# An identity made on GpSimd, first transposes in the order of the loads, larger q and k loads, and half of v's loads issued by GpSimd

## The chip, the cores and the metric

The kernel runs on one core of a Trainium2 chip. The metric is device time in microseconds (us) of one execution; lower is better. The kernel before took 1226.99 us (median of three runs, 1224.92 to 1231.88).

## What is computed

Attention over chunks of 64 tokens, then a mixture of eight experts in which tokens are assigned in the order of their logits up to a capacity, then a dense layer of three weights. Only the first part is touched by the change:

```python
# q, k, v: (8 batches, 8 heads, 576 tokens, 64), float32; 9 chunks of 64 tokens
scores = scale * q_c @ k_c.T            # within each chunk of 64 tokens
attn   = softmax(scores)                # max subtracted, sum + 1e-9
x      = (attn @ v_c)                   # to (4608 tokens, 512)
logits = x @ w_gate                     # 4608 x 8
# tokens take experts in the order of the sorted logits, 576 per expert
y[mask_e]  = relu(x[mask_e] @ w1[e]) @ w2[e]
out = max(relu(y @ m1), y @ m2, y @ m3) @ m_out
```

## The kernel before

The 72 chunks (8 batches of 9) are worked on in 36 iterations of two chunks, all eight heads at once. Four iterations share one unit `u` of eight chunks: there are nine units. For each unit, q and k are loaded by 128 partitions (16 per chunk, four tokens in each, 1 KB in one piece per head); v by 64 partitions per chunk, with 256 bytes in one piece. Since a unit of eight chunks can begin in one batch and end in the next, a q or k load of a unit is issued in one or two pieces (`pieces`, L37). `load_qk(u, part)` (L46) loads four heads of k or q or both; `load_v(u, part)` (L58) loads two chunks of v in four transfers of 64 KB, of which one is issued by GpSimd where `u` is above 0.

TensorE needs q and k with the head's 64 elements on the partitions. `trans(nm, u, n)` (L85) turns two of the eight heads by four transposes against the identity `ident`, into one of two PSUM buffers `pT`; `evac` (L97) copies the result in two halves, by ScalarE and VectorE, into `QT`. Transposes `n` = 0 and 1 read heads 0 to 3, `n` = 2 and 3 heads 4 to 7.

Before the loop, unit 0 is loaded (`load_qk(0, 0)`, `load_qk(0, 1)`), then parts of v of unit 0 and of q and k of unit 1 by turns (L78 to L83); the eight transposes of unit 0 run with k and q by turns (L204 to L208). In the loop (L213), iteration `i` loads a quarter of v of unit `i // 4 + 1` and a quarter of q and k of unit `i // 4 + 2`, and runs the scores of `i` (L112), its maximum, difference and exponential, the transposes of one quarter of unit `i // 4 + 1`, the attention times v of `i - 1` (L161), and scaling, store and transposes of x of `i - 2` (L168, L170, L179). Logits come every fourth iteration (L191, L200). q's and k's buffers are double, so a load of unit `u + 1` has to wait until unit `u - 1` is transposed.

The order of the work on each engine is that of the program; each engine works through its own list in order. SyncE issues q, k and most of v; GpSimd issues the stores of x and a quarter of v; ScalarE issues `w_gate` and two transfers for the identity.

The identity is made in `Router.__init__` (L295 to L298): VectorE writes a matrix with ones in its first column, ScalarE stores it to memory (`unit`) and reads it back with a row pitch of 127, which puts the ones on the diagonal. `Router.consts` (L300) has GpSimd make the router's constants; among them `dif` (L322), column minus row, and its comparison with zero (L334). It is called before `attention`, so it comes ahead of the memsets of two of v's three buffers (L76, L77) in GpSimd's list.

Of the kernel before, what the change touches and what calls it, by code (L numbers as in the profile page):

```python
# [7 lines left out]
F32 = mybir.dt.float32  # L8
# [5 lines left out]
OP = mybir.AluOpType  # L14
# [3 lines left out]
B, H, S, D = 8, 8, 576, 64  # L18
# [5 lines left out]
NU = G // 4  # L24
# [1 line left out]
BIG = 1.5e38  # L26


def attention(ctx, tc, q, k, v, wg_in, xd, L, ident, early, mark):

    nc = tc.nc
    C = ctx.enter_context(tc.tile_pool(name="ac", bufs=1))
    P = ctx.enter_context(tc.tile_pool(name="aw", bufs=2))
    PS = ctx.enter_context(tc.tile_pool(name="aps", bufs=2, space=PSUM))
    QK, QT, KBT, PT, PSS, MX, A, R, PA, AT, PX, X, PY, XT, LS = ({} for _ in range(15))

    def pieces(u):  # L37
        r, j = [], 0
        while j < 8:
            b, c = divmod(8 * u + j, 9)  # L40
            n = min(8 - j, 9 - c)
            r.append((j, n, b, c))
            j += n
        return r

    def load_qk(u, part, nms="kq"):  # L46

        for nm in nms:
            if part == 0:
                QK[nm, u] = P.tile([128, H, 4 * D], F32, name="in" + nm)  # L50
            src, h = (k if nm == "k" else q), 4 * part
            for j, n, b, c in pieces(u):
                nc.sync.dma_start(
                    QK[nm, u][16 * j:16 * (j + n), h:h + 4],
                    bass.AP(tensor=src.tensor, offset=src.offset + (b * H + h) * S * D + c * 64 * D,
                            ap=[[4 * D, 16 * n], [S * D, 4], [1, 4 * D]]))

    def load_v(u, part):  # L58

        t = VB[u % 3]  # L60
        for j in (2 * part, 2 * part + 1):
            b, c = divmod(8 * u + j, 9)
            for s in range(2):
                (nc.gpsimd if u and j % 2 and s else nc.sync).dma_start(
                    t[s * 64:(s + 1) * 64, j, :, s, :],
                    bass.AP(tensor=v.tensor, offset=v.offset + b * H * S * D + s * S * D + c * 64 * D,
                            ap=[[D, 64], [2 * S * D, 4], [1, D]]))

    load_qk(0, 0)
    load_qk(0, 1)  # L70
    wg = C.tile([128, 4, 32], F32, name="wg")
    nc.vector.memset(wg, 0.0)
    nc.scalar.dma_start(wg[:, :, :8], wg_in.rearrange("(a p) e -> p a e", p=128))
    VB = [C.tile([128, 8, 4, 2, 64], F32, name="vb%d" % i) for i in range(3)]
    for t, eng in ((VB[0], nc.vector), (VB[1], nc.gpsimd), (VB[2], nc.gpsimd)):
        eng.memset(t[0:64, :, :, 1, :], 0.0)  # L76
        eng.memset(t[64:128, :, :, 0, :], 0.0)  # L77
    load_v(0, 0)  # L78
    load_qk(1, 0)
    load_v(0, 1)  # L80
    load_v(0, 2)
    load_qk(1, 1)
    load_v(0, 3)  # L83

    def trans(nm, u, n):  # L85

        mark(nm + "T")
        if n == 0:
            QT[nm, u] = P.tile([128, 4, 8, 64], F32, name=nm + "T")
        pt = PS.tile([128, 2, 2, 128], F32, name="pT")  # L90
        PT[nm, u, n] = pt
        for a in range(2):
            for w in range(2):
                h = 4 * (n // 2) + 2 * a + n % 2
                nc.tensor.transpose(pt[:, a, w, :], QK[nm, u][:, h, w * 128:w * 128 + 128], ident)  # L95

    def evac(nm, u, n, r, eng):  # L97
        mark(nm + "E")
        s, h0 = n % 2, 2 * (n // 2)
        src = PT[nm, u, n][r * 64:r * 64 + 64].rearrange("p a w t -> p a t w")  # L100
        dst = QT[nm, u][s * 64:s * 64 + 64, h0:h0 + 2].rearrange("p a j (i w r) -> p a (j i) w r", w=2, r=2)[:, :, :, :, r]
        (nc.vector.tensor_copy if eng else nc.scalar.copy)(dst, src)

    def scores(g):
        mark("scores")
        u, h = divmod(g, 4)
        PSS[g] = PS.tile([128, 2, 512], F32, name="pS", bufs=1)[:, :, :256].rearrange("p s (a i) -> p a s i", a=4)
        for hp in range(4):
            for c in range(2):
                for s in range(2):  # L110
                    o, to = slice(s * 64, s * 64 + 64), slice(c * 64, c * 64 + 64)
                    nc.tensor.matmul(PSS[g][to, hp, s], QT["q", u][o, hp, 2 * h + c], QT["k", u][o, hp, 2 * h + c],  # L112
                                     start=True, stop=True, tile_position=(s * 64, c * 64))
# [51 lines left out]
    def scale(g):  # L165
        mark("scale")
        X[g] = P.tile([128, 8, 64], F32, name="x", bufs=3)
        nc.vector.tensor_tensor(X[g], PX[g].rearrange("p a (s i) -> p (a s) i", s=2),  # L168
                                R[g][:, :, None].to_broadcast([128, 8, 64]), op=OP.mult)
        nc.gpsimd.dma_start(xd[g * 128:(g + 1) * 128, :], X[g].rearrange("p h d -> p (h d)"))  # L170
# [30 lines left out]
        nc.vector.tensor_reduce(L[:, 4 * j + w0:4 * j + w1, :],  # L201
                                pl[:, w0:w1, :, :8].rearrange("p w a e -> p w e a"), op=OP.add, axis=AX.X)

    for n in range(4):  # L204
        for nm in "kq":
            trans(nm, 0, n)
            for r in range(2):
                evac(nm, 0, n, r, r)  # L208

    def on(j):  # L210
        return 0 <= j < G

    for i in range(G + 2):  # L213
        u, n = i // 4 + 1, i % 4
        tr = u < NU
        if tr:
            load_v(u, n)
        if u + 1 < NU:
            load_qk(u + 1, n // 2, "kq"[n % 2])
        if on(i):  # L220
            scores(i)
        if on(i - 2):
            scale(i - 2)
        if on(i):
            smax(i)
        if on(i - 1):
            att_t(i - 1)
            att_c(i - 1)
            sums(i - 1, 0)
        if tr:  # L230
            trans("q", u, n)
            evac("q", u, n, 0, 0)
            trans("k", u, n)
            evac("k", u, n, 0, 0)
        if on(i):
            ssub(i)
        if tr:
            evac("k", u, n, 1, 1)
        if on(i):
            expo(i)  # L240
        if i == G + 1:
            logit1(8, 0, 3)
        if on(i - 2):
            x_t(i - 2)
        if tr:
            evac("q", u, n, 1, 0)
        if on(i - 1):
            pv(i - 1)
            sums(i - 1, 1)
            sums(i - 1, 2)  # L250
        if i >= 7 and (i - 4) % 4 == 3 and i < G:
            logit2((i - 4) // 4)
        if i >= 6 and (i - 3) % 4 == 3 and i < G:
            logit1((i - 3) // 4)
        if on(i - 2):
            x_c(i - 2)
        if i == G + 1:
            early()
            logit2(8, 0, 3)
            logit1(8, 3, 4)  # L260
            logit2(8, 3, 4)
# [3 lines left out]
class Clock:  # L265
# [4 lines left out]
    def __init__(s):  # L270
        s.pe = s.dve = 0
# [12 lines left out]
class Router:  # L284

    def __init__(s, ctx, tc, mark, scratch):
        s.tc, s.mark, s.clock = tc, mark, Clock()
        nc = s.nc = tc.nc  # L290
        C = s.C = ctx.enter_context(tc.tile_pool(name="rc", bufs=1))
        s.L = C.tile([128, G, E], F32, name="L")
        s.ident = C.tile([128, 128], F32, name="ident")

        nc.vector.memset(s.ident, 0.0)  # L295
        nc.vector.memset(s.ident[:, 0:1], 1.0)
        nc.scalar.dma_start(scratch, s.ident)
        nc.scalar.dma_start(s.ident, bass.AP(tensor=scratch.tensor, offset=scratch.offset, ap=[[127, 128], [1, 128]]))  # L298

    def consts(s, tmp):  # L300
        nc, C = s.nc, s.C

        def io(shape, pat, base=0, cm=0, name=None):
            t = C.tile(shape, F32, name=name)
# [9 lines left out]
                       allow_small_or_imprecise_dtypes=True)  # L314
# [3 lines left out]
                       allow_small_or_imprecise_dtypes=True)  # L318
        s.row = io([128, 1], [[0, 1]], cm=1, name="row")
        s.w8 = io([128, E], [[-1, E]], base=E, name="w8")  # L320
        dif = tmp.tile([128, 128], F32, name="dif")
        nc.gpsimd.iota(dif, pattern=[[1, 128]], base=0, channel_multiplier=-1, allow_small_or_imprecise_dtypes=True)  # L322
        s.tri = C.tile([128, 128], BF, name="tri")
        nc.gpsimd.tensor_scalar(s.tri, dif, 0.0, None, op0=OP.is_gt)

# [298 lines left out]
def kernel(ctx, tc, q, k, v, w_gate, w1, w2, m1, m2, m3, m_out, out, mark=lambda n: None):  # L624
    nc = tc.nc
    ctx.enter_context(tc.manual_schedule())
    dram = ctx.enter_context(tc.tile_pool(name="dram", bufs=1, space=bass.MemoryType.DRAM))
    xd = dram.tile([NT, DM], F32, name="xd")
# [2 lines left out]
    mo = dram.tile([F2, DM], F32, name="mo")  # L631
    wda = dram.tile([9 * 128, 2, 768], F32, name="wda")
    wdb = dram.tile([9 * 128, 2, 1024], F32, name="wdb")
    unit = dram.tile([128, 128], F32, name="unit")
    rt = Router(ctx, tc, mark, unit)
    with ExitStack() as c2:
        consts = c2.enter_context(tc.tile_pool(name="tmp", bufs=1))
        rt.consts(consts)
        attention(c2, tc, q, k, v, w_gate, xd, rt.L, rt.ident, rt.early, mark)
    ring = ctx.enter_context(tc.tile_pool(name="ring", bufs=10))  # L640
    P = rt.W = ctx.enter_context(tc.tile_pool(name="mw", bufs=1))
    c3 = ExitStack()
# [300 lines left out]
    for r in range(E):  # L943
# [53 lines left out]
        for d in range(4):  # L997
# [3 lines left out]
            for hf in range(2):  # L1001
                tk = slice(hf * 288, hf * 288 + 288)
                n = 0
# [193 lines left out]
```

## Time and profile before

| what | value |
|---|---|
| median of three runs | 1226.99 us |
| profiled execution | 1226.38 us |
| its span, first to last instruction | 1224.6 us |
| busy in the span | TensorE 1173.0 us (96%), VectorE 846.3 (69%), ScalarE 415.2 (34%), GpSimd 263.8 (22%) |
| granted TensorE clock, mean | 0.989 |
| HBM traffic | 197 GB/s over the span |

Busy time counts an engine as busy while an instruction of it runs; the span is cut from the first to the last instruction, and the execution's time is 1.8 us longer. Attention fills the first 170 us of the span, the router's first round the time up to about 205 us, the experts and the dense layer the rest.

### The profile page before, as it was taken

To read this page: it belongs to the slowest core of one execution; us is meant where nothing else is said; L and a number is where in the kernel's file an instruction comes from. 1 tells how busy PE (TensorE), PEld (TensorE's weight loads), DVE (VectorE), ACT (ScalarE), POOL (GpSimd) and SP (SyncE) were. 2 spreads that over 40 slices of the span, in tenths; PEclk is the share of its full clock that TensorE was granted. 3 is DMA by queue.
4 is the path that set the end of the run, shared out by engine and by line. 5 is a ranking of instruction groups with operands and counts; after the bars stand their busy time and mean duration, and the time that the engine had idled before them with its cause. 6 is when DMAs were issued, how large, how long until landed. Compare 5 with 4: busy or idle time off the path is not lost.

```text
span 1224.6 us, 23432 instructions
## 1 busy us (share of the span) xinstructions
PE 1173.0 (96%) x9485; PEld 1093.1 (89%) x9485; DVE 846.3 (69%) x1684; ACT 415.2 (34%) x673; POOL 263.8 (22%) x381
## 2 busy tenths in 40 slices
PE   5999978999999999999899999999999999999998
PEld 4787745899999998999899998998998998998996
DVE  5888876877788889888954466566566565565561
ACT  4888832233333332334423113113113113113111
POOL 6232211010135343544760001001001001002002
PEclk9999987999999999999999999999999999999999
DMA  9999915263655565757674564674663763763651
GB/s 210 250 262 248 228 53 164 80 227 96 202 179 191 169 202 173 233 167 255 210 257 176 215 253 174 232 263 150 258 256 139 266 241 138 267 252 135 220 202 52
DMA packets 148781, 243.11 MB, mean 199 GB/s; under 512 B 39490, under 2 KB 111938, under 8 KB 141762
## 3 DMA queue, kind: packets, MB, share of 16 engines
q1 hardware_dynamic: 129234, 184.05, 47.2%
q0 software_dynamic: 14016, 47.98, 11.6%
q10 hardware_dynamic: 5424, 9.59, 2.2%
q8 instruction: 75, 1.23, 0.4%
q14 instruction: 32, 0.26, 0.1%
HBM read 195.12 MB, written 46.47 MB: 197 GB/s over the span
## 4 chain that ended last, share of the span: by engine, by line
PE 41%; issue 36%; DVE 10%; DMA 8%; POOL 2%; SPq 1%; ACT 1%; POOLq 1%; DVEq 0%; ACTq 0%
PE acc L1007 14%; PE acc L964 13%; DMA inq<-in_q_dram 4%; PE py L1045 2%; POOL out_dram L1129 2%; DMA vb<-in_v_dram 2%; DVE chunk L693 2%; PE px L1045 2%; PE pz L1045 2%; PE pX L161 1%; PE pxt L747 1%; PE pT L95 1%; PE po L1121 1%; DVE hlo L984 1%; DVE ge L469 1%
## 5 line engine op out<-in xcount | busy, mean ns | idle before, releaser
L1007 PE MATMUL acc<-hhi,chunk 128*128 128x288 f32 x1024 | 211.1, 300 | 1.2 <-DVE hlo L984 1.2
L964 PE MATMUL acc<-xhi,chunk 128*128 128x288 f32 x1024 | 206.4, 300 | 3.9 <-DVE hlo L984 3.2
L964 PEld LDWEIGHTS acc<-xhi,chunk 128*128 128x128 f32 x1024 | 160.3, 188 | 6.0 <-DVE hlo L984 4.1
L1007 PEld LDWEIGHTS acc<-hhi,chunk 128*128 128x128 f32 x1024 | 162.7, 188 | 1.8 <-DVE hlo L984 1.5
L1007 PE MATMUL acc<-hlo,chunk 128*128 128x288 f32 x512 | 151.0, 295 | 1.0 <-DVE hlo L984 0.9
L1121 PE MATMUL po<-chunk,h 128*128 128x512 f32 x648 | 149.3, 390 | 0.0
L1129 POOL DMA_INDIRECT out_dram<-ot,ia x36 | 35.4, 985 | 521.1 <-ACT ot L1127 519.6
L1121 PEld LDWEIGHTS po<-chunk,h 128*128 128x128 f32 x648 | 121.5, 188 | 24.8
L964 PE MATMUL acc<-xlo,chunk 128*128 128x288 f32 x512 | 143.0, 295 | 0.0
L1045 PE MATMUL px<-xb,wa 128*128 128x384 f32 x648 | 129.9, 334 | 0.7 <-ACT ys L1014 0.7
L1045 PE MATMUL py<-xt,wb 128*128 128x384 f32 x648 | 129.8, 334 | 0.0
L1045 PEld LDWEIGHTS px<-xb,wa 128*128 128x128 f32 x648 | 113.9, 188 | 1.3 <-ACT ys L1014 1.0
L1045 PEld LDWEIGHTS py<-xt,wb 128*128 128x128 f32 x648 | 114.0, 188 | 0.5
L1066 ACT CAST h<-best 128x384 fp32r<-128x384 f32 x72 | 37.0, 514 | 198.0 <-DVE best L1064 121.3
L1007 PEld LDWEIGHTS acc<-hlo,chunk 128*128 128x128 f32 x512 | 96.0, 188 | 1.4 <-DVE hlo L984 1.4
L964 PEld LDWEIGHTS acc<-xlo,chunk 128*128 128x128 f32 x512 | 93.4, 188 | 0.0
L976 ACT ACTIVATE hhi<-acc 128x576 fp32r<-128x576 f32 x64 | 41.8, 652 | 144.6 <-PE acc L964 121.4
L693 DVE TENSOR_TENSOR chunk<-raw,chunk 128x1024 fp32r<-128x1024 f32 x67 | 88.2, 1320 | 2.7 <-ACT chunk L686 2.7
L1081 ACT COPY tmp<-px 128x384 f32<-128x384 f32 x54 | 25.9, 480 | 146.2 <-PE px L1045 146.2
L723 POOL DMA_INDIRECT xg<-xd,idx x40 | 41.9, 1049 | 153.7 <-DVE ohe L612 65.5
L686 ACT CAST chunk<-raw 128x1024 fp32r<-128x1024 f32 x67 | 69.7, 1046 | 8.9 <-ACT ys L1014 6.9
L984 DVE SCALAR_TENSOR_TENSOR hlo<-acc,hhi 128x576 fp32r<-128x576 f32 x64 | 48.2, 753 | 34.5 <-ACT hhi L976 34.3
(207 smaller groups left out, 2012.4 us busy)
## 6 DMA issues: line engine op xcount, KB each, us to landing
wb<-wdb SPq DMA_DIRECT2D x54, 1024.0 KB, 4.9
wa<-wda SPq DMA_DIRECT2D x54, 768.0 KB, 5.9
raw<-in_moe_w_dram SPq DMA_DIRECT2D x64, 512.0 KB, 4.5
xd<-x POOLq DMA_DIRECT2D x36, 256.0 KB, 5.3
yd<-ys ACTq DMA_DIRECT2D x32, 288.0 KB, 3.1
wdb<-pair POOLq DMA_DIRECT2D x18, 512.0 KB, 5.2
yraw<-yd SPq DMA_DIRECT2D x12, 768.0 KB, 7.5
vb<-in_v_dram SPq DMA_DIRECT2D x112, 64.0 KB, 5.8
```

What stands on the lines that cost most here:

```text
L686: nc.scalar.copy(hi, raw)
L693: nc.vector.tensor_tensor(lo, raw, hi.bitcast(F32), op=OP.subtract)
L723: nc.gpsimd.indirect_dma_start(out=g, out_offset=None, in_=xd[:, :], in_offset=bass.IndirectOffsetOnAxis(ap=rt.idx[r][:, t:t + 1], axis=0))
L964: nc.tensor.matmul(acc[:, hf, :288], w[a][:, dc, o:o + 128], x[:, dc, tk], start=n == 0, stop=n == 11)
L976: nc.scalar.activation(hv, acc[:, :, :288], AF.Relu)
L984: nc.vector.scalar_tensor_tensor(hl[:, f].rearrange("p (a t) -> p a t", a=2), acc[:, :, :288], 0.0, hv.bitcast(F32), op0=OP.max, op1=OP.su ...
L1007: nc.tensor.matmul(acc[:, hf, :288], w[a][:, f, :], x[:, f, tk], start=n == 0, stop=n == 23)
L1045: nc.tensor.matmul(dst, w[:, dc, o, a], XO[x][:, c, dc], start=start and n == 0, stop=stop and n == 5, skip_group_check=True)
L1066: nc.scalar.copy(hpart(g, i, j)[0], M)
L1081: nc.scalar.copy(U[g, 1], XB[g])
L1121: nc.tensor.matmul(PO[t], h[:, x, t % 6 * 128:t % 6 * 128 + 128], w[a][:, f % 2], start=f == 0 and n == 0, stop=f == 5 and n == 2)
L1129: st = nc.gpsimd.indirect_dma_start(out=out, out_offset=bass.IndirectOffsetOnAxis(ap=ia[:, t:t + 1], axis=0), in_=ot, in_offset=None)
```

## The change

The identity is made by GpSimd as the first thing after its start: an iota of column minus row and a comparison with zero (`unit`). The round trip through memory goes, and the other constants (`consts`) are called from inside `attention`, after the memsets of v's buffers. `load_qk` now takes one of q and k, a first head and a number of heads: unit 0 and 1 are still loaded by four heads, later units by eight at once, k in the first and q in the third iteration of four. Unit 1's second half moves ahead of the third quarter of unit 0's v. In `load_v`, both transfers of the upper half of the partitions are issued by GpSimd where `u` is above 0, two of four. The first transposes run as k 0, k 1, q 0, q 1, k 2, k 3, q 2, q 3.

```diff
-    def load_qk(u, part, nms="kq"):
-        for nm in nms:
-            if part == 0:
-                QK[nm, u] = P.tile([128, H, 4 * D], F32, name="in" + nm)
-            src, h = (k if nm == "k" else q), 4 * part
-            for j, n, b, c in pieces(u):
-                nc.sync.dma_start(
-                    QK[nm, u][16 * j:16 * (j + n), h:h + 4],
...
+    def load_qk(nm, u, h, n):
+        if h == 0:
+            QK[nm, u] = P.tile([128, H, 4 * D], F32, name="in" + nm)
+        src = k if nm == "k" else q
+        for j, m, b, c in pieces(u):
+            nc.sync.dma_start(
+                QK[nm, u][16 * j:16 * (j + m), h:h + n],
...
-                (nc.gpsimd if u and j % 2 and s else nc.sync).dma_start(
+                (nc.gpsimd if u and s else nc.sync).dma_start(
...
-    load_qk(0, 0)
-    load_qk(0, 1)
+    for h in (0, 4):
+        for nm in "kq":
+            load_qk(nm, 0, h, 4)
     wg = C.tile([128, 4, 32], F32, name="wg")
     nc.vector.memset(wg, 0.0)
-    nc.scalar.dma_start(wg[:, :, :8], wg_in.rearrange("(a p) e -> p a e", p=128))
     VB = ...
+    nc.scalar.dma_start(wg[:, :, :8], wg_in.rearrange("(a p) e -> p a e", p=128))
+    consts()
     load_v(0, 0)
-    load_qk(1, 0)
+    for nm in "kq":
+        load_qk(nm, 1, 0, 4)
     load_v(0, 1)
+    for nm in "kq":
+        load_qk(nm, 1, 4, 4)
     load_v(0, 2)
-    load_qk(1, 1)
     load_v(0, 3)
...
-    for n in range(4):
+    for n in (0, 2):
         for nm in "kq":
-            trans(nm, 0, n)
-            for r in range(2):
-                evac(nm, 0, n, r, r)
+            for i in (n, n + 1):
+                trans(nm, 0, i)
+                for r in range(2):
+                    evac(nm, 0, i, r, r)
...
-        if u + 1 < NU:
-            load_qk(u + 1, n // 2, "kq"[n % 2])
+        if u + 1 < NU and n % 2 == 0:
+            load_qk("kq"[n // 2], u + 1, 0, 8)
...
-        nc.vector.memset(s.ident, 0.0)
-        nc.vector.memset(s.ident[:, 0:1], 1.0)
-        nc.scalar.dma_start(scratch, s.ident)
-        nc.scalar.dma_start(s.ident, bass.AP(tensor=scratch.tensor, offset=scratch.offset, ap=[[127, 128], [1, 128]]))
+    def unit(s, tmp):
+        s.dif = tmp.tile([128, 128], F32, name="dif")
+        s.nc.gpsimd.iota(s.dif, pattern=[[1, 128]], base=0, channel_multiplier=-1, allow_small_or_imprecise_dtypes=True)
+        s.nc.gpsimd.tensor_scalar(s.ident, s.dif, 0.0, None, op0=OP.is_equal)
...
-        rt.consts(consts)
-        attention(c2, tc, q, k, v, w_gate, xd, rt.L, rt.ident, rt.early, mark)
+        rt.unit(consts)
+        attention(c2, tc, q, k, v, w_gate, xd, rt.L, rt.ident, lambda: rt.consts(consts), rt.early, mark)
```

## Rows read from the trace of the kernel before

**Rows 1.** Stretches: us, busy us (instructions) by engine, clock, DMA share, GB/s.
```profile
40.00:130.00 90.00, 86.39 (x1453) 71.51 (x1452) 77.87 (x159) 77.75 (x136) 25.79 (x44) 1.00 1.14 252
...
175.00:200.00 25.00, 17.36 (x149) 8.45 (x150) 17.18 (x77) 2.98 (x3) 1.54 (x2) 0.50 0.22 69
```

**Rows 2.** Chain of waits: start us, us, what (a DMA lasts to its landing).
```profile
0.77 4.04 DMA ink<-in_k_dram
...
4.82 6.04 DMA vb<-in_v_dram
10.86 1.09 PE pT L95 x4
...
13.38 1.13 PE pT L95 x4
```

**Rows 3.** Timeline of ScalarE, start: start us, us, instruction.
```profile
5.04 0.34 ACTq L298 DMA_DIRECT2D ident<-unit  x1
```

**Rows 4.** Waits of SyncE, 0 to 20 us: us, times, longest.
```profile
SPq L53 <- DMA ident<-unit: 3.6, 1, 3.6
```

**Rows 5.** Timeline of TensorE [idle <-releaser]; last, its waits, 30 to 152 us.
```profile
37.53 0.63 PE L95 MATMUL pT<-ident,inq 128*128 128x128 f32 x4 [0.88 <-PE pA L148]
...
48.50 0.69 PE L112 MATMUL pS<-kT,qT 64*64 64x64 f32 x32
...
132.26 0.69 PE L112 MATMUL pS<-kT,qT 64*64 64x64 f32 x32
...
148.14 0.69 PE L112 MATMUL pS<-kT,qT 64*64 64x64 f32 x32
...
PE pT L95 <- DMA inq<-in_q_dram: 3.1, 5, 1.1
```

**Rows 6.** DMA issues at 2.38 and 31.05: KB, us to landing.
```profile
inq<-in_q_dram SPq DMA_DIRECT2D x1, 512.0 KB, 7.4
...
inq<-in_q_dram SPq DMA_DIRECT2D x1, 384.0 KB, 6.4
```

**Rows 7.** SyncE's timeline from 103 us; last, two steps of the chain there.
```profile
103.22 1.16 SPq L53 DMA_DIRECT2D inq<-in_q_dram  x2
104.42 3.15 SPq L64 DMA_DIRECT2D vb<-in_v_dram  x3
108.47 0.85 SPq L53 DMA_DIRECT2D ink<-in_k_dram  x2
109.37 2.98 SPq L64 DMA_DIRECT2D vb<-in_v_dram  x3
...
103.22 7.83 DMA inq<-in_q_dram
...
111.06 0.60 SPq L64
```

**Rows 8.** Timeline of GpSimd, start.
```profile
3.59 0.23 POOL L322 IOTA dif<- 128x128 f32 x1
...
6.30 0.54 POOL L334 TENSOR_SCALAR blk<-dif 128x128 f32<-128x128 f32 x1
...
18.57 2.14 POOL L64 DMA_DIRECT2D vb<-in_v_dram  x3
```

**Rows 9.** Timeline: VectorE's first copy of a transpose, and later transposes.
```profile
12.63 0.69 DVE L102 COPY kT<-pT 64x512 f32<-64x512 f32 x1 [6.97 <-ACT kT L102]
...
22.50 0.60 PE L95 MATMUL pT<-ident,ink 128*128 128x128 f32 x4
```

**Rows 10.** DMA totals, 3 to 10 us and 17.4 to 18.6 us.
```profile
DMA packets 3596, 2.35 MB, mean 335 GB/s; under 512 B 1377, under 2 KB 3596, under 8 KB 3596
...
DMA packets 918, 0.22 MB, mean 183 GB/s; under 512 B 918, under 2 KB 918, under 8 KB 918
```

**Rows 11.** GpSimd's group of x stores, 40 to 130 us: busy, mean ns | idle before.
```profile
L170 POOL DMA_DIRECT2D xd<-x x22 | 12.4, 561 | 65.7 <-DVE x L168 60.6 <-DMA inq<-in_q_dram 2.6 <-DMA vb<-in_v_dram 2.5
```

**Rows 12.** One stretch between the first loads and the next, as rows 1.
```profile
10.30:13.00 2.70, 1.94 (x8) 1.57 (x8) 0.37 (x1) 0.80 (x2) 2.62 (x8) 1.00 0.36 53
```

More of the change, by code (lines that the diff above doesn't have):

```diff
@@ L26, with attention @@
 BIG = 1.5e38
-def attention(ctx, tc, q, k, v, wg_in, xd, L, ident, early, mark):
+def attention(ctx, tc, q, k, v, wg_in, xd, L, ident, consts, early, mark):
     nc = tc.nc
@@ L44, in pieces @@
         return r
-    def load_qk(u, part, nms="kq"):
-        for nm in nms:
-            if part == 0:
-                QK[nm, u] = P.tile([128, H, 4 * D], F32, name="in" + nm)
-            src, h = (k if nm == "k" else q), 4 * part
-            for j, n, b, c in pieces(u):
-                nc.sync.dma_start(
-                    QK[nm, u][16 * j:16 * (j + n), h:h + 4],
-                    bass.AP(tensor=src.tensor, offset=src.offset + (b * H + h) * S * D + c * 64 * D,
-                            ap=[[4 * D, 16 * n], [S * D, 4], [1, 4 * D]]))
+    def load_qk(nm, u, h, n):
[5 more added lines that the diff above has]
+                QK[nm, u][16 * j:16 * (j + m), h:h + n],
+                bass.AP(tensor=src.tensor, offset=src.offset + (b * H + h) * S * D + c * 64 * D,
+                        ap=[[4 * D, 16 * m], [S * D, n], [1, 4 * D]]))
     def load_v(u, part):
@@ L284, with __init__ @@
 class Router:
-    def __init__(s, ctx, tc, mark, scratch):
+    def __init__(s, ctx, tc, mark):
         s.tc, s.mark, s.clock = tc, mark, Clock()
@@ L293, in __init__ @@
         s.ident = C.tile([128, 128], F32, name="ident")
-        nc.vector.memset(s.ident, 0.0)
-        nc.vector.memset(s.ident[:, 0:1], 1.0)
-        nc.scalar.dma_start(scratch, s.ident)
-        nc.scalar.dma_start(s.ident, bass.AP(tensor=scratch.tensor, offset=scratch.offset, ap=[[127, 128], [1, 128]]))
+    def unit(s, tmp):
+        s.dif = tmp.tile([128, 128], F32, name="dif")
+        s.nc.gpsimd.iota(s.dif, pattern=[[1, 128]], base=0, channel_multiplier=-1, allow_small_or_imprecise_dtypes=True)
+        s.nc.gpsimd.tensor_scalar(s.ident, s.dif, 0.0, None, op0=OP.is_equal)
     def consts(s, tmp):
-        nc, C = s.nc, s.C
+        nc, C, dif = s.nc, s.C, s.dif
         def io(shape, pat, base=0, cm=0, name=None):
@@ L320, in consts @@
         s.w8 = io([128, E], [[-1, E]], base=E, name="w8")
-        dif = tmp.tile([128, 128], F32, name="dif")
-        nc.gpsimd.iota(dif, pattern=[[1, 128]], base=0, channel_multiplier=-1, allow_small_or_imprecise_dtypes=True)
         s.tri = C.tile([128, 128], BF, name="tri")
@@ L633 @@
     wdb = dram.tile([9 * 128, 2, 1024], F32, name="wdb")
-    unit = dram.tile([128, 128], F32, name="unit")
-    rt = Router(ctx, tc, mark, unit)
+    rt = Router(ctx, tc, mark)
     with ExitStack() as c2:
         consts = c2.enter_context(tc.tile_pool(name="tmp", bufs=1))
-        rt.consts(consts)
-        attention(c2, tc, q, k, v, w_gate, xd, rt.L, rt.ident, rt.early, mark)
+        rt.unit(consts)
+        attention(c2, tc, q, k, v, w_gate, xd, rt.L, rt.ident, lambda: rt.consts(consts), rt.early, mark)
     ring = ctx.enter_context(tc.tile_pool(name="ring", bufs=10))
```

## The prediction

> **What bounds the kernel now.** I read the busy time by stretches first [rows 1]. From 40 to 130 us TensorE is busy 86.39 of 90 us at a granted clock of 1.00. So attention is TensorE's own work wherever nothing holds it up, and the question is only where it is held up: before its first instruction, and in the 3.6 us that are missing from 40 to 130.
>
> The start of the chain of waits [rows 2] shows the first. TensorE's first transposes begin at 10.86 us, although k's first half landed at 0.77 + 4.04 = 4.81. The view calls the transfer between them "vb", but the thing that came late is the identity: ScalarE can only fetch it back from memory from 5.04 on [rows 3], and SyncE, whose next issue uses that fetch's completion semaphore again, waits 3.6 us for "ident" [rows 4]. The first transposes start as it lands.
>
> The second shows in the starts of the scores, one per iteration [rows 5]. Four iterations that nothing delays take 148.14 - 132.26 = 15.88 us. The five groups of four before them, 48.50 to 132.26, take 83.76, which is 4.4 us more than 5 x 15.88; TensorE's waits give the reason, q's loads, 3.1 us in five times, up to 1.1. So loads cost between 3.1 and 4.4 us there; I take 4.3, as no other wait comes near them. At 37.53 there is one more of 0.88: q's piece issued at 31.05 landed 6.4 later, at 37.4 [rows 6].
>
> Why are those loads late? SyncE's list [rows 7] has its answer in one stretch: the load issued at 103.22 lands at 103.22 + 7.83 = 111.05, and at 111.06 SyncE issues again. Between the two it issued exactly eight (two q, three v, two k, one v). Each of SyncE's and ScalarE's issues takes one of eight completion semaphores and waits for the landing of the one eight before. Five issues per iteration at 6 to 8 us each from issue to landing, eight at a time, is 5 x 6.3 / 8 = 3.9 us per iteration, just TensorE's 15.88 / 4 = 3.97. SyncE is therefore never ahead, and any slow landing reaches TensorE.
>
> **The change, part by part.**
>
> *Identity on GpSimd.* Removed: two memsets, two ScalarE issues, the round trip through memory. Added at the head of GpSimd: an iota of 0.23 and a comparison like the one at 6.30, 0.54 [rows 8], done within 2 us even if GpSimd starts 1 us into the span. Then k's landing at 4.81 is the last thing that the first transposes wait for: 10.86 becomes 4.85, **-6.0 us**. The memsets and constants behind it are the same work as before in another order, so GpSimd still comes to its first v load near 18.57 [rows 8]; unit 1's v is used first after iteration 4's scores, so that costs nothing. If GpSimd's constants slowed VectorE's copies beside them, four copies of 0.69 [rows 9] in the path could double, 2.8 us. GpSimd was at work without a break until that v load, beside those same copies, so I take nothing.
>
> *Order of the first transposes.* Two PSUM buffers, and tile j waits for VectorE's copy of tile j-2: 13.38 - 10.86 = 2.5 us per two tiles [rows 2]. That pace stays. From 4.85 the second matrix is wanted at 7.4, the third load at 9.9, the fourth at 12.5; the fourth lands at 2.38 + 7.4 = 9.8 [rows 6], the others in equal steps after 4.81, at about 6.5 and 8.1. The new order costs and gains nothing by itself. The first transposes take 1.1 us per four [rows 2], those at 22.50 0.6 [rows 9]. I let the change of speed move along with them. Should it stay where it is, the first two iterations run slow, up to 4 us (7 us of work, of which half waits for other engines anyway).
>
> *What is late next.* q of the third unit, needed at iteration 4. Without its wait it would be needed at 37.53 - 0.88 - 6.0 = 30.65. When does it come? SyncE's prologue is 4 qk, 4 v, 4 qk, 4 v, 4 qk, 8 v, then 2 v, 2 k, 4 v, 2 q. By issue: the 9th to 12th wait for the landings of the first loads, the last at 9.8, instead of all four for the identity until just before 10.86, so the second unit's first halves are out by about 10.8; then 18 v at 0.65 and 8 qk pieces at 0.5 to 0.55 (0.43 to 0.65 each in [rows 7]) come to 15.9: q is out at about 26. It moves twice the bytes of the piece that landed 6.4 later [rows 6], so 32. By bytes: 6.3 MB of q and k at the 335 GB/s that k and q alone reached and 1.8 MB of v at 183 [rows 10] are 18.8 + 10.0 us, from 3.2 on (the first landing less its 1.6): 32.0. Both say 32, a wait of 1.4. Place 37.53 moves to 32.1: **-5.4 us** are left of the 6.0. The range of this step is 30.65 (nothing waits) to 35.5 (the same 8.1 MB at the 252 GB/s of rows 1, 32.3 us).
>
> *Eight heads at once, half of v from GpSimd.* SyncE's issues per four iterations fall from 20 (12 v, 8 qk pieces) to 12 (8 v, 4 pieces of double bytes): 12 x 0.65 = 7.8 us of 15.88, and eight in flight now reach over two and a half iterations. The transfers must still fit: per iteration 524 KB of q and k at 335 GB/s is 1.56 us, 262 KB of v at 183 is 1.43, 262 KB of x in packets no smaller than q's is at most 0.78 at 335 [rows 10]; together 3.77 against TensorE's 3.97. GpSimd's v loads rise from four to eight per group: 8 x 0.71 (2.14 for three in [rows 8]) + 4 x 0.561 [rows 11] = 7.9 us of 15.88. They stand in the queue between one x store and the next; the store waits for VectorE anyway (60.6 us in 22 times), so 1.4 us of issues before it are hidden; uncovered they would cost at most the 0.7 added per iteration. Then q is needed whole two iterations after its place in the program, where now its halves have three. But SyncE is held only by the buffer of two units before, free one iteration ahead of the group, and by then has 7.8 us of issues to do in 15.9: q goes out about 1 us into the group, lands by 12 and is needed at 17. So the stalls go: **-4.3 us**. Bounds: 0 (all stay) to -4.7.
>
> [...] The DMA queues' share reads 1.14 from 40 to 130 us [rows 1]: no free engine is visible. [...] The row on eight in flight says that bandwidth was not what was short; the fit of 3.77 in 3.97 decides, and it is close.
>
> *After attention* all moves along. The granted clock is 0.50 from 175 to 200 us [rows 1], while the router keeps TensorE waiting. If its fall and rise do not move along exactly, 4 us more or less of TensorE's work there at the other level make up to 2 us either way; I take 0.
>
> **Sum.** -5.4 - 4.3 = -9.7 on a span of 1224.6. The profiled execution took 1226.4, so 1216.7; the median shown, 1226.99, is 0.6 above it. I say **1217**.
>
> **Rivals.**
>
> *Half of it.* The start's gain is eaten at iteration 4: q lands at 35 or later, or the first iterations stay slow. Then -1.5 to -2.5 there, -4.3 later: about 1220.5. For it: q's bytes are due 5.4 us sooner at rates met only without a mix. Against: 2.7 us from 10.3 to 13.0 ran at 53 GB/s [rows 12], an empty stretch that the identity alone made.
>
> [...]
>
> *q whole comes late in every group (slower).* Place: the wait of the first transpose of each unit. If SyncE does not get ahead and issues q in iteration 2 of 4, it has two iterations and 1.1 us, 9.0 us, to land. Seven loads are concerned; with x us of lateness each, 7x stands against the 9.7: it is slower than before from x = 1.4, that is a landing 10.4 us after issue. The longest now is 7.8 for half the bytes, plus 1.6 for the rest at 335 GB/s and 0.6 for the second issue: 10.0, just short; at 12 us x = 3, and 1226.4 - 9.7 + 21 = 1238. Against: 12 issues instead of 20, so SyncE has time to be ahead.
>
> **How the numbers follow.** A measurement of this kernel tells about 0.5% (6 us) from no change. Forecast 0.56 (own range 1213.5 to 1220); half of it 0.20, split evenly between faster and same; engines bound 0.17, same; q late 0.07, slower. Faster 0.67 (0.56 + 0.10, and a little), same 0.25, slower 0.08. The range: down to 1212.5 (6.0 + 4.7 kept, 2 us of the clock), up to 1224.5, which takes in the bandwidth case and leaves out the slower one.
>
> **What will show it.** The first transposes begin at 4.9 and the first scores near 14; iteration 4's q transposes at 32, and the waits of transposes for q after that near zero; four iterations take 15.9 throughout; iteration 31's scores begin near 138.4 instead of 148.14; SyncE idle before each k load. Wrong, if q's loads still end TensorE's waits, if groups take over 16.3, or if SyncE's issues still follow the landing of the eighth before.

## The result: slower by 0.85%, and the profile after

The kernel after takes 1237.78 us (median of nine runs, 1234.71 to 1241.09), the kernel before 1226.99 (nine runs, 1224.83 to 1231.88): a ratio of 1.0085, 95% interval 1.0064 to 1.0105. The forecast of 1217 is 21 us off, and the time lies outside its range. The profiled execution took 1241.09 us, the longest of the nine; its span is 14.6 us longer than that of before. The page's totals for it:

```profile
span 1239.2 us, 23433 instructions
...
PE 1178.7 (95%) x9485; PEld 1099.2 (89%) x9485; DVE 850.3 (69%) x1682; ACT 414.8 (33%) x673; POOL 282.8 (23%) x414
...
PEclk8799996899999999999999999999999999999999
```

TensorE is busy 5.7 us more with the same work, so part of the loss is work at a lower clock: there are dips in the first and second of the 40 slices, where before has none, and in the seventh and eighth, where before has its own in the sixth and seventh. Its timeline (start, us, instruction, idle before and what ended it), beside [rows 5]:

```profile
14.13 1.06 PE L115 MATMUL pS<-kT,qT 64*64 64x64 f32 x18
...
29.42 0.53 PE L115 MATMUL pS<-kT,qT 64*64 64x64 f32 x18
...
42.59 1.08 PE L98 MATMUL pT<-ident,inq 128*128 128x128 f32 x4 [10.87 <-DMA inq<-in_q_dram]
...
47.01 0.69 PE L115 MATMUL pS<-kT,qT 64*64 64x64 f32 x32
...
85.62 0.27 PE L115 MATMUL pS<-kT,qT 64*64 64x64 f32 x2 [1.23 <-issue]
...
160.43 0.69 PE L115 MATMUL pS<-kT,qT 64*64 64x64 f32 x32
```

And the chain of waits, beside [rows 2] (a DMA lasts to its landing):

```profile
0.77 4.30 DMA ink<-in_k_dram
...
5.20 1.10 PE pT L98 x4
...
27.98 0.27 SPq L52
...
28.29 14.16 DMA inq<-in_q_dram
42.45 0.14 issue
42.59 1.94 PE pT L98 x8
```

The starts of the scores of single iterations divide the 14.6 us:

| place | before | after | difference |
|---|---|---|---|
| first scores | 20.08 | 14.13 | -5.95 |
| iterations 0 to 3 (to the start of 4) | 14.27 | 15.29 | +1.0 |
| iteration 4 | 5.64 | 17.59 | +11.95 |
| iterations 5 to 30 (start of 5 to start of 31) | 108.15 | 113.42 | +5.3 |
| after that | | | +2.3 |

The first gain is there. Then TensorE waits 10.87 us for q of the third unit, issued at 28.29 and landed at 42.45, which costs more than was won. Stretches of the kernel after, with the columns of [rows 1]:

```profile
20.00:42.50 22.50, 10.79 (x190) 9.05 (x187) 12.11 (x24) 10.53 (x19) 8.55 (x15) 0.79 1.15 225
...
40.00:46.60 6.60, 4.01 (x24) 3.71 (x26) 0.97 (x3) 2.61 (x5) 0.00 (x0) 0.50 1.18 177
40.00:130.00 90.00, 80.62 (x1282) 66.64 (x1283) 68.04 (x137) 68.83 (x121) 33.82 (x57) 0.96 1.10 232
...
128.70:132.10 3.40, 3.40 (x24) 3.07 (x24) 1.07 (x3) 2.72 (x5) 0.47 (x1) 0.50 0.41 90
...
217.40:224.20 6.80, 6.13 (x28) 5.56 (x27) 3.38 (x6) 3.18 (x6) 0.00 (x0) 0.50 0.63 183
```

The first row is the wait: the 16 engines have a share of 1.15 throughout, at 225 GB/s. Of the 10.5 us by which q lands behind the forecast 32, 2.3 are its issue (28.29 instead of 26) and 8.2 its transfer (14.16 instead of 6). The clock of 0.50 behind it is a second price: iteration 4's first transposes take 1.08 us per four where [rows 9] has 0.60.

TensorE's waits from 0 to 175 us (us, times, longest) and SyncE's from 40 to 130:

```profile
PE pT L98 <- DMA inq<-in_q_dram: 10.9, 1, 10.9
...
PE pS L115 <- issue: 3.1, 3, 1.2
PE pT L98 <- issue: 1.8, 1, 1.8
PE pX L164 <- issue: 1.5, 2, 1.0
...
PE pA L151 <- issue: 0.4, 1, 0.4
...
SPq L52 <- PE pT L98: 25.5, 4, 9.3
```

After iteration 4 no transpose waits for q, and SyncE, which followed the landing of the eighth before [rows 7], now waits for a buffer to come free. In their place TensorE has 6.8 us of idle time in seven times that no wait explains ("issue"), where before had 0.3.

### The profile page after: what moved, and what is told of

Its sections match the earlier page's. It is cut to its first block, busy times and chain, and to the rows that moved or that the text cites. A ratio compares the mean times of both kernels' runs of the same rounds, so it can differ in the third digit from the quotient of the medians.

```text
span 1239.2 us, 23433 instructions
## 1 busy us (share of the span) xinstructions
PE 1178.7 (95%) x9485; PEld 1099.2 (89%) x9485; DVE 850.3 (69%) x1682; ACT 414.8 (33%) x673; POOL 282.8 (23%) x414
## 4 chain that ended last, share of the span: by engine, by line
PE 45%; issue 36%; DVE 11%; DMA 3%; POOL 2%; ACT 1%; POOLq 1%; DVEq 0%; SPq 0%; ACTq 0%
PE acc L1008 13%; PE acc L965 11%; PE pX L164 3%; PE pT L98 3%; PE py L1046 2%; DVE chunk L694 2%; POOL out_dram L1130 2%; PE pS L115 2%; PE pA L151 2%; PE px L1046 2%; PE pz L1046 2%; PE pxt L748 1%; DMA inq<-in_q_dram 1%; PE po L1122 1%; PE pY L182 1%
## 5 line engine op out<-in xcount | busy, mean ns | idle before, releaser
L694 DVE TENSOR_TENSOR chunk<-raw,chunk 128x1024 fp32r<-128x1024 f32 x67 | 92.9, 1390 | 2.5 <-ACT chunk L687 2.2
L985 DVE SCALAR_TENSOR_TENSOR hlo<-acc,hhi 128x576 fp32r<-128x576 f32 x64 | 48.2, 753 | 31.7 <-ACT hhi L977 31.5
```

Of the source, the lines that this page charges most:

```text
L694: nc.vector.tensor_tensor(lo, raw, hi.bitcast(F32), op=OP.subtract)
L985: nc.vector.scalar_tensor_tensor(hl[:, f].rearrange("p (a t) -> p a t", a=2), acc[:, :, :288], 0.0, hv.bitcast(F32), op0=OP.max, op1=OP.su ...
```

## The experiments

Iteration 4's wait, the issue idle (31 to 175 us) and the median us from issue to landing of SyncE's v loads (50 to 130 us) are each from the run's profile. A time without an interval is one run.

| kernel | us | ratio to before | wait for q at iteration 4 | issue idle | v landing |
|---|---|---|---|---|---|
| before | 1226.99 | | 0.9 | 0.3 | 5.8 |
| after | 1237.78 | 1.0085 [1.0064, 1.0105] | 10.9 | 6.8 | 8.7 |
| start alone | 1224.85 | 0.998 [0.9964, 0.9996] | 4.0 | 0.2 | 6.1 |
| start + half of v | 1229.96 | 1.0013 [0.9994, 1.0033] | 3.2 | 3.3 | |
| start + eight heads | 1236.14 | 1.0072 [1.0044, 1.01] | 10.7 | 4.7 | 7.6 |
| after, unit 2 by four heads | 1237.29 | 1.0091 [1.0061, 1.0122] | 1.4 | 4.9 | |
| after, loads split in place | 1234.62 | | 8.8 | 6.0 | 7.4 |
| after, v later | 1234.91 | | 6.2 | 6.3 | 8.4 |
| start alone, v later | **1221.13** | **0.995 [0.9933, 0.9966]** | 0 | 1.1 | 5.9 |
| before, v later | 1223.4 | 0.9969 [0.9956, 0.9982] | 0 | 0 | 6.1 |

**The parts.** The start alone: both other parts undone.

```diff
-        if u + 1 < NU and n % 2 == 0:
-            load_qk("kq"[n // 2], u + 1, 0, 8)
+        if u + 1 < NU:
+            load_qk("kq"[n % 2], u + 1, 4 * (n // 2), 4)
...
-                (nc.gpsimd if u and s else nc.sync).dma_start(
+                (nc.gpsimd if u and j % 2 and s else nc.sync).dma_start(
```

> Only the start of the change: identity on GpSimd, the new prologue and the new order of the first transposes; q and k by four heads and a quarter of v from GpSimd as in the kernel before. Theory (the whole q of the third unit is what came late, behind everything else in flight): its first half is needed first and lands near 33, TensorE waits under 3 us at iteration 4 instead of 10.9, and the time is about 1221 to 1224 us, faster than before by 3 to 6. Rival (the transfer engines are full, so that an earlier start only meets a later wait): 1225 to 1229, same as before. Rival (the new start itself hurts): over 1232.

Of some 6 us at the first scores 0.2% of the time is left. TensorE's waits from 31 to 175 us say where it went:

```profile
PE pT L98 <- DMA inq<-in_q_dram: 5.0, 3, 4.0
PE pT L98 <- issue: 0.2, 1, 0.2
```

The 4.0 are at iteration 4 (34.55): the start moved by 6 us and q's landing by 3.0 (34.41 instead of 37.44). Its issue came 3.8 us sooner (27.28 instead of 31.05), and its transfer took 7.1 us instead of 6.4. The time lies between the theory's range and that of the first rival, and the wait of 4.0 speaks for the rival.

The first hunk alone (start and half of v), and the second alone (start and eight heads):

> The changed kernel with q and k of the loop by four heads again, half of v still from GpSimd. Theory: as the start alone at iteration 4, and SyncE with four issues per iteration instead of five gets ahead of eight in flight: 1218 to 1222 us, waits of transposes for q near zero after iteration 4. Rival (engines full): no better than the start alone, 1225 to 1229. Rival (half of v from GpSimd is what hurts): 1234 or more, with TensorE idle times put down to issue as in the changed kernel, some 6 us of them before 175.

> The changed kernel with a quarter of v from GpSimd, q and k by eight heads. Theory (whole q is late): the wait at iteration 4 stays near 10 us and the time is 1234 to 1240. Rival (GpSimd's v loads take the engines from q): the wait at iteration 4 falls under 5 us, 1226 to 1230.

Eight heads at once bring nearly all of the loss (1.0072 of 1.0085) and the wait at iteration 4. Half of v on GpSimd brings no wait for q beyond the start's own, but 3.3 us of issue idle against 0.2, and takes the start's gain away. Its time of 1229.96 misses the theory's range (1218 to 1222) and lies between those of the two rivals.

**Why does q come late at iteration 4?** First, unit 2 alone loaded by four heads, later units by eight:

```diff
-        if u + 1 < NU and n % 2 == 0:
+        if u == 1:
+            load_qk("kq"[n % 2], u + 1, 4 * (n // 2), 4)
+        elif u + 1 < NU and n % 2 == 0:
             load_qk("kq"[n // 2], u + 1, 0, 8)
```

> The changed kernel, but unit 2 alone (the one whose q came late at iteration 4) by four heads in the order k, q, k, q; later units by eight. Theory: the wait of 10.9 us falls to under 4 and the clock's fall in it goes, so 9 to 13 us come back of the changed kernel's loss: 1225 to 1229; what is left over the start alone are later idle times put down to issue (about 5 us), which belong to the large loads. Rival (the lateness only moves to the next unit): a wait of 5 us or more at iteration 8, 1232 or more.

The rival held. The time stays (1237.29), and the wait stands four iterations further on, at the first unit that is loaded whole:

```profile
60.03 1.09 PE L98 MATMUL pT<-ident,inq 128*128 128x128 f32 x4 [8.95 <-DMA inq<-in_q_dram]
```

So it is not the start's crowd of loads. Is it the size of the transfer or its place in the order? Each load of eight heads issued as two of four, in the same place:

```diff
-            load_qk("kq"[n // 2], u + 1, 0, 8)
+            load_qk("kq"[n // 2], u + 1, 0, 4)
+            load_qk("kq"[n // 2], u + 1, 4, 4)
```

> The changed kernel with each load of eight heads issued as two of four heads one after the other, at the same place in the program. Theory (bytes ahead of q decide, in program order): the first half of q is what iteration 4 waits for, 0.5 MB earlier, some 2 us, and more issues hold SyncE back; the wait goes from 10.9 to 7 to 9 us. Rival (the size of the single load decides): it falls to about 3, as with four heads per iteration.

The wait is 8.8 us, as the theory had it: the place decides most of it. All of k goes ahead of all of q, and SyncE has more to issue ahead of it. Then v ahead of q: no loads of v in the loop, and the loop's loads of v two iterations later.

```diff
-        if tr:
-            load_v(u, n)
...
```

The part of the edit that is left out sets v's other two buffers to zero.

> The changed kernel without the loads of v for units 1 to 8 (the buffers hold zeros, so x of those units is zero): 36% of the loop's transfer time goes, order and size of q's and k's loads stay. Theory (the transfer engines are full, and whole q waits behind the bytes ahead of it): the wait at iteration 4 falls from 10.9 us to under 2, no later wait for q, and the idle times put down to issue (6.8 us of TensorE's before 175 in the changed kernel) fall under 1, since a refill of instructions has less to queue behind. Rival (q is issued too late in the program, whatever is in flight): the wait at iteration 4 stays over 6 us. Rival for the issue times (they belong to the large loads by themselves): 3 us or more of them stay.

```profile
36.36 0.87 PE L102 MATMUL pT<-ident,inq 128*128 128x128 f32 x3 [4.75 <-issue]
```

```diff
-        if tr:
-            load_v(u, n)
+        if 0 <= i - 2 < 4 * (NU - 1):
+            load_v((i - 2) // 4 + 1, (i - 2) % 4)
```

> The changed kernel with v's loads two iterations later. Theory (bytes ahead of whole q): v of unit 1 no longer stands ahead of q except what GpSimd and SyncE issue from iteration 2 on, 0.75 MB less, the wait at iteration 4 goes from 10.9 to 6 to 8 us; time 1230 to 1235. Rival: no change in the wait.

Without v the wait falls from 10.9 to 4.75 us (TensorE's timeline names "issue", but q, issued at 23.82, landed at 36.27, just ahead), between the theory's 2 and the rival's 6; the other issue idle falls to 1.1, and the time is 1229.86. With v later it is 6.2, as the theory had it. How the wait comes about shows in the piece of q that is waited for (times from the start of the span; TensorE is ready when it has nothing left to do but that transpose):

| kernel | issued | to landing | landed | TensorE ready |
|---|---|---|---|---|
| start alone (four heads) | 27.28 | 7.13 | 34.41 | 30.5 |
| after | 28.29 | 14.16 | 42.45 | 31.7 |
| loads split in place | 31.92 | 7.65 | 39.57 | 30.9 |
| v left out | 23.82 | 12.45 | 36.27 | 31.6 |
| v later | 25.66 | 11.98 | 37.64 | 31.5 |

Split in place, q's first half lands in 7.65 us, but goes out 3.6 us later. Loading q whole doubles the time to landing, and most of that stays without v: 12.45 of 14.16 us (k of the next unit, issued at 27.88, is in flight beside it there). What v's loads add is for the larger part their issues: without them q goes out 4.5 us sooner, about the time of six issues at 0.77 (SyncE's ten v issues from 15.54 us on take 7.66), and lands 1.7 sooner after that; with v later it is 2.6 and 2.2. So v ahead of q counts in SyncE's list as well as on the engines. How the rest divides into q's own bytes and those of k these runs do not show.

**A better order.** The same edit on the start alone, and on the kernel before:

> The start of the change alone (four heads, a quarter of v from GpSimd), with v's loads of the loop two iterations later in the program (three iterations ahead of their use instead of five). Theory (engines full, and v's bytes stand ahead of q's though they are needed later; after iteration 31 the engines are nearly idle): 0.5 MB less ahead of q of unit 2, the wait at iteration 4 goes from 4.0 to about 2 us, the later waits for q (4.5 us) mostly go: 1218 to 1222. Rival (v comes late in their place): waits of attention times v for vb, and no gain, 1224 to 1228.

> The kernel before with v's loads two iterations later and nothing else (the identity through memory, the old order). It tells what the start is worth once the transfers in the loop are in the order of their use. Theory (the engines' order was the bound, and 6 us of the earlier start can now be kept): the waits for q go and 1222 to 1225 us remain, 2 to 5 us slower than the new start with the same loads (1221.13, interval of its ratio 0.9933 to 0.9966). Rival (the later v gives it all and the start nothing): 1220 to 1222, no different from that kernel.

The first is faster than before and after (0.995); both times lie in the ranges of their theories. Its scores of iteration 31, and those of the second, beside 148.14 [rows 5]:

```profile
141.06 0.69 PE L115 MATMUL pS<-kT,qT 64*64 64x64 f32 x32
```

```profile
143.61 0.58 PE L112 MATMUL pS<-kT,qT 64*64 64x64 f32 x24
```

Putting v behind q, in the order of their use, is worth 4.5 us by itself at that place; the start then adds 2.6. The two times' intervals overlap, so the start's part rests on the profiles alone. In the faster kernel TensorE's waits for loads and issue from 31 to 175 us come to 1.3 us:

```profile
PE pS L115 <- issue: 1.1, 1, 1.1
...
PE pT L98 <- DMA inq<-in_q_dram: 0.2, 1, 0.2
```

**What is the issue idle?** It shows before scores, products and transposes alike. Ahead of the end of one such idle in the kernel after (start 85.62, above) the DMA queues show, in the stretch 82.8 to 83.0 us, one packet of 16 KB of instructions (packets, MB, share):

```profile
q8 instruction: 1, 0.02, 37.3%
```

It begins at 82.9 and lasts 1.2 us; the idle ends 1.5 later. In all runs but the last two together there are 40 issue idles over 0.2 us after 37 us, and 38 of them end 1.3 to 1.8 us after the end of such a packet, while packets come some 8 us apart. The page counts them over the span:

```profile
q8 instruction: 75, 1.23, 0.4%
```

TensorE's own records in that trace are 9485 weight loads, 9485 matmuls and 228 waits and drains, 19198 in all: 256 to a packet, to within two records. And counted in blocks of 256 in the order of their start, all these idles but one, and the three of the last two runs too, stand at the same place of a block (the 194th or 195th record), whatever the instruction there: 42 of 43. The exception is 0.23 us before a transpose of q in the start alone. From these counts I infer that TensorE waits there for the next block of its own instructions; no record names what a packet holds. The theory: the packet comes late when many transfers are in flight. Starting from the better order, eight heads alone and half of v alone (the two hunks of the first diff above, each taken back by itself):

> New start, v two iterations later, q and k by eight heads, a quarter of v from GpSimd. Beside the kernel with four heads (1221.1, TensorE's idle times put down to issue 1.1 us, v's median landing 5.9 us) and the changed kernel with v later (1234.9; 6.2; 8.4) it tells which of the two parts does it. Theory (large loads fill the queues, and both q and the refills of instructions come late): wait at iteration 4 of 5 us or more, issue times of 3 us or more, landing over 7 us, 1230 to 1235. Rival (half of v from GpSimd does it): near 1222.

```profile
PE pS L115 <- issue: 3.1, 1, 3.1
...
PE pX L164 <- issue: 2.2, 2, 1.8
```

> New start, v two iterations later, q and k by four heads, half of v from GpSimd. Theory (large loads are the cause): no wait over 2 us at iteration 4; SyncE ahead with four issues per iteration, so more in flight than with a quarter: issue times of 1 to 4 us, 1221 to 1226. Rival (half of v from GpSimd does it): wait at iteration 4 of 5 us or more, issue times over 4, 1229 or more.

```profile
PE pS L115 <- issue: 3.9, 3, 2.0
...
PE pX L164 <- issue: 0.8, 1, 0.8
```

Either part brings it back: 5.3 us (1233.25 us in all; the wait for q at iteration 4 is 8.2), and 4.7 us (1224.87; no wait for q, but one of 1.1 for v). The first is as its theory had it; in the second the time is in the theory's range, the idle above its 1 to 4 us. With them v from SyncE lands 7.6 and 7.9 us after issue, against 5.9. Next, three unused loads of 1 MB added to the better order, by SyncE at iterations 9, 17 and 25:

```diff
+        if i in (9, 17, 25):
+            extra(i)
...
```

`extra` loads 1 KB of k for each of 128 partitions and eight heads into a tile that nothing reads.

> New start, four heads, quarter of v, v two iterations later (1221.1), and beside it three loads of 1 MB that nothing uses, issued by SyncE at iterations 9, 17 and 25. It raises the suspected cost alone. Theory (TensorE's refill of instructions, a transfer itself, comes late when much is in flight): an idle time put down to issue of 0.5 to 2 us within two iterations after at least two of the three, where that kernel has none in 45 to 100 us; waits for q may come too. Rival (the idle times are of another kind, of the order of the program or of GpSimd): waits for q alone.

```profile
PE pT L98 <- DMA inq<-in_q_dram: 11.9, 4, 4.1
...
PE pS L115 <- issue: 0.3, 1, 0.3
```

A miss for the theory: the time was 1235.7, TensorE waited for q, 3.1 to 4.1 us after each, and the issue idle was 0.3 us. A late packet can come in during a wait for q, so this run could hide what it was to show; in one place it did. After the first extra load TensorE passed the place of the block at 65.0 us, and the next packet began at 74.4, the latest of all; the wait of 3.5 us for q (to 69.22) lies between. The last two keep the bytes and change who issues the half of v: ScalarE, whose issues name the same eight completion semaphores as SyncE's (465 issues of both in the trace of before, 405 in that of after), where GpSimd's name eight others (180 and 212); and GpSimd with three quarters instead of half.

```diff
-                (nc.gpsimd if u and s else nc.sync).dma_start(
+                (nc.scalar if u and s else nc.sync).dma_start(
...
+                (nc.gpsimd if u and (s or j % 2) else nc.sync).dma_start(
```

> As the version with the start, v two iterations later and half of v on GpSimd (which had 4.7 us of TensorE idle put down to issue, v from SyncE landing 7.9 us after issue), but that half of v is issued by ScalarE. ScalarE's issues take their completion semaphores from the same eight as SyncE's, so fewer transfers are in flight at once, for the same bytes. Theory (a block of TensorE's instructions is fetched by the same 16 engines and comes late when many transfers are in flight): v lands 5.5 to 6.5 us after issue and the issue idle from 31 to 175 us falls to 0 to 1.5 us. Rival (the idle comes with taking v's issues off SyncE, whoever does them): it stays at 3.5 to 6 us. ScalarE's own issues may hold its exponentials: waits of TensorE for ScalarE are then to be counted apart, and the time may be 1222 to 1235 us.

> As the version with the start, v two iterations later and half of v on GpSimd (4.7 us of issue idle; v from SyncE landing 7.9 us after issue), but three of four v transfers are issued by GpSimd. Same bytes, still more in flight beside SyncE's eight, which are then mostly q and k. Theory (depth of the transfers in flight delays the fetch of TensorE's instructions): v from SyncE lands 8.5 us or more after issue, the issue idle is 5 us or more, each idle ends 1.4 to 1.8 us after a 16 KB packet of instructions, time 1225 to 1232 us. Rival (the idle of 4.7 us was chance in one profile): it falls to 0 to 2 us.

With ScalarE there is no issue idle, but q waits of 8.6 us in four times, which leaves the same doubt (1234.29 us; the packets, below, decide it). With three quarters (1229.8 us), from 31 to 175 us:

```profile
PE pS L115 <- issue: 7.4, 3, 3.5
PE pT L98 <- issue: 1.7, 1, 1.7
```

The 1.7 is at iteration 4, 2.5 us after a packet's end and at the 107th record of a block, the place of q's transpose where "issue" was q before; the other three, 7.4 us, end 1.4 to 1.6 after one. So the sizes go up with v's share on GpSimd for the same bytes: 1.1, 4.7 and 7.4 us for a quarter, a half and three quarters; one profile each. That is the theory's side (5 or more); the rival, that chance made the 4.7, forecast 0 to 2. The traces hold no landings of v for these last two runs, so that part of their expectations stays untested.

How late the packets are can be read without the idles: from TensorE's passing the place in one block to the beginning of the packet that ends ahead of the next (medians, 31 to 150 us; the last five rows are the better order with one thing changed).

| kernel | us to the packet | issue idle |
|---|---|---|
| before | 3.0 | 0.3 |
| after | 4.8 | 6.8 |
| start alone, v later (the better order) | 2.8 | 1.1 |
| with eight heads | 4.6 | 5.3 |
| with half of v from GpSimd | 4.6 | 4.7 |
| with three quarters | 4.5 | 7.4 |
| with half of v from ScalarE | 1.3 | 0 |
| with three extra loads | 3.6 | 0.3 |

In none of the 16 profiles did TensorE pass a place sooner than 1.3 us after its packet's end. In the ScalarE run the packets come soonest, at 1.3 us, so q's waits hid nothing there: no packet was late.

## Why the prediction was wrong, step by step

*Identity on GpSimd, -6.0*: right. The matrix is ready at 1.76 us, the transposes begin at 5.20 with k's landing at 5.07, and the first scores are 5.95 earlier.

*The order of the first transposes, 0, up to 4*: +1.0 by iteration 4. The granted clock was 0.50 from 12.6 to 19.4 us, so the change of speed did not move along with the start. This is not the same each time: in the profile of the start alone the clock was 1.00 from 11.4 to 31.9 us, and the same iterations took 14.23 us (14.27 before).

*q of the third unit, "q is out at about 26 ... so 32"*: this is the step that failed. It went out at 28.29 (the prediction's own terms, 10.8 + 15.9, come to 26.7) and landed at 42.45, 14.16 later instead of 6. The DMA totals from 3 to 42.5 us show both halves of the error:

```profile
DMA packets 14784, 9.80 MB, mean 248 GB/s; under 512 B 8074, under 2 KB 14398, under 8 KB 14782
```

The sum had 8.1 MB in 28.8 us, at 335 GB/s for q and k and 183 for v [rows 10]. Neither is the rate of the mix. The 183 is of 1.2 us of v alone, and the 335 of the first loads, not of q and k alone as the prediction says: v's first four went out in that stretch, too. At 248 GB/s the 8.1 MB take 32.7, +3.9 us. And the 1.7 MB left out of the sum take 6.9 more: three stores of x (0.8 MB), GpSimd's v of the iterations after (0.4; its first six loads are in the sum), and v and k that SyncE issued behind q. Neither alone makes the loss: the range's far end of 35.5 had the slow rate, but not the bytes. The second estimate, "twice the bytes of the piece that landed 6.4 later", was no second witness: whole q took 14.16 us with v in flight beside it, and without v, with k of the next unit beside it, still 12.45.

*Eight heads at once and half of v from GpSimd, "so the stalls go: -4.3"*: half right. SyncE did get ahead, and behind iteration 4 no wait for q was left, where before had 3.1 us. But the fit that was to decide, 3.77 us of 3.97 per iteration, rests on the same unmixed rates: at the 252 GB/s of [rows 1] the same 1.05 MB take 4.16, and do not fit. The count of eight is right: in the trace of before 152 issues of SyncE and ScalarE up to 130 us come behind the first eight, all on the same eight completion semaphores; 144 wait on their own one, the other eight for a buffer to come free, and none of the 114 whose earlier landing on that semaphore the trace holds begins ahead of it. The eight of SyncE's in flight now hold loads of up to 1 MB, and half of v comes on top of them from GpSimd. The engines moved no more for it (239 GB/s from 50 to 130 us, 253 before), and v's landings came later, 8.7 us after issue instead of 5.8. The instruction packets came later with them, 4.8 us after TensorE's passing the place instead of 3.0, and 6.8 us of issue idle took the waits' place. After one of the idles, that before 128.53, the clock was 0.50 for 3.4 us, which cost an estimated 1.7 us (half of them). In all it is +5.3 instead of -4.3.

*After attention, 0, bounds of 2 either way*: +2.3, just outside. The clock's fall did not move along: TensorE waited 2.07 us for the gathered tokens, and the clock was 0.50 from 217.4 to 224.2, on the experts' first matmuls.

*The range.* Its lower end does not follow from its terms: 6.0 + 4.7 + 2 off the 1226.4 is 1213.7, not 1212.5.

*The rivals.* "q whole comes late in every group (slower)" had the place, the first transpose of a unit. That its time of 1238 is nearly the measured one is chance, as the count is another: not 3 us in seven groups but 10.9 once, at the first unit that is loaded whole. From then on SyncE is ahead. Its deciding landing of 10.4 us after issue was put aside with a longest of 10.0 from one piece's rate; it was 14.16. "Engines bound" (0.17) describes the start alone: if the loads end as before but for the nearly empty 2.7 us of [rows 12], 1226.4 becomes about 1224, an estimate, and 1224.85 was measured. GpSimd's issues brought no bandwidth: with half of v there in the better order the engines moved 254 GB/s from 50 to 130 us, with a quarter 259.

*What stays open.* That TensorE's idle is a late fetch of instructions is inferred from when it ends (38 of 40 times 1.3 to 1.8 us after a packet's end), from its place in a block of 256 records (42 of 43), and from how late the packets begin (4.8 us in the kernel after, 3.0 before). No run shows when a fetch is asked for, whose instructions a packet holds, or what it waits for before it begins. GpSimd's issuing is not needed for it: eight heads alone, with GpSimd's quarter as before, bring 5.3 us. For the half of v, many transfers in flight and GpSimd's own way of issuing were not told apart.

## What to carry to other kernels

Where the DMA engines are busy throughout, as here at a share of 1.15, work a landing out from all bytes that move up to it on every queue, at the rate measured in that mix: 9.80 MB at 248 GB/s gave q's landing, and the unmixed rates and another piece's time to landing missed it by 10 us. Count the issues that stand ahead in the issuing engine's list, too. Splitting loads by when their parts are due is a priority order, and merging them gave that order up here: first put loads in the order of their use. An earlier start alone was worth only as much as the loads behind it could follow (2 to 3 of its 6 us).

## What the runs showed of the hardware that was not expected

Three waits of TensorE cost more than themselves. After the 10.87 us wait (to 42.59) the clock stayed at 0.50 to 46.7 us; in the extra-load run it was 0.50 from 69.0 to 72.4 us, behind the wait to 69.22, and 0.51 from 106.5 to 109.9, behind one of 3.1 to 4.1 us.

The trace of after has one 16 KB instruction packet for every 256 of TensorE's records (75 for 19198). Of TensorE's idles over 0.2 us with no wait in the profile to show for them, 41 of 43 ended 1.3 to 1.8 us after the end of such a packet. With 17 to 19 such packets between 31 and 175 us in each run, these idles came to from 0 (before, with v later) to 7.4 us (three quarters of v on GpSimd).
